# Blocks of 448 columns: sorting where PSUM is read instead of where operands are written

## The chip, the cores and the metric

The kernel runs on one core of a Trainium2 chip. The metric is the device time of one execution in microseconds (us). Three runs of the kernel before gave a median of 1079.95 us (1079.29 to 1080.52).

## The reference

```python
def _attn_ref(x, filt_r, filt_i):             # x: (2, 3008, 256)
    X = np.fft.rfft(x, axis=1)
    Y = X * (filt_r + 1j * filt_i)[None, :, :]
    return np.fft.irfft(Y, n=x.shape[1], axis=1).astype(np.float32)

def _moe_ref(x, w_in, w_out):                 # x: (6016, 256), w_in: (256, 2048), w_out: (2048, 256)
    h = x @ w_in
    g = np.where(h > 0.0, h, np.exp(np.minimum(h, 0.0)) - 1.0)
    return g @ w_out

def _moe2_ref(x, w_in, w_out):
    h = x @ w_in
    g = h * np.clip(h + 3.0, 0.0, 6.0) / 6.0
    return g @ w_out

# reference: x -> _attn_ref -> rows (6016, 256) -> _moe_ref -> _moe2_ref
```

A circular convolution over each of two sequences of 3008 rows, and then two two-layer networks, with an ELU and with a hard swish between their layers. The weights come as float64 and everything is float32.

## The kernel before

**Transforms.** The transform of 3008 = 47 x 64 points is done as matmuls: a step of 47 points (s1), one of 64 (s2), the product with the filter (`mult`, L203 to L211), and the two steps back (i2, i1). The first sequence is transformed in the prologue with float32 matmuls. The second sequence's transform runs beside the first network: there s1, s2 and i2 split each operand into a high and a low part (`split_in`, L957) and do three matmuls (`mm3`, L83 to L86: high x high, low x high, high x low). These read their moving operand contiguously: 16 x 3 matmuls in s1, 12 x 3 in s2 and 12 x 3 in i2. Their banks are read by `s1_evac` (L185), `mult` (L208, L209) and `i2_evac` (L222).

**Blocks.** The 6016 tokens stand as columns: twelve blocks, per sequence five of 512 and one of 448 (blocks 5 and 11). The 2048 hidden units are 16 chunks of 128. In the first network blocks 0 to 2 run side by side, then blocks 3, 4, 5, 6 and 11 one after the other (`SINGLES`), then the pairs (7, 8) and (9, 10). The second network runs six pairs; the last is (5, 11), the only one that is 448 wide. A single block's chunk is one unit: two halves of the first layer (`g1`), the ELU on its bank (L499 to L503), the split of its result (`g_split`, L506), and two output halves (`g2`), 12 matmuls in all. `g2` of a unit comes three units behind its `g1`. A pair's step takes two chunks for two blocks with seven products in place of eight (`prod`), evacuates them (`copy`, L631; `add`, L637), applies the function (`relu`, L648; `gate`, L658), splits (`high`, L668; `low`, L673) and multiplies with the second layer's weights (`second`). Each round of 16 chunks is eight such groups.

**Splits.** Every moving operand is split: ScalarE copies it into a rounded high part, VectorE subtracts that to get the low part. The lines are L101 and L102 for single blocks and block inputs, L105 (in `moved`) with L567 and L673 for pairs, L80 and L81 for transforms.

**Reading in pairs.** The network's matmuls read their moving operand with `shuffled`: element 0, element n/2, element 1, element n/2 + 1 and so on. In a 512 block the result is left in that order: it passes through four layers, and the output pass (L609 to L619) undoes it by reading a bank in steps of 16. In a 448 block order is kept at every layer: the split writes its halves in steps of n/2 (`paired`, `placed`), so that reading in pairs gives the original order, and banks are read contiguously.

**What sets the order.** Each engine takes its instructions in the order in which the program lists them. The list is written by hand: a prologue string, then a loop over units with lists of jobs before and after each (`pre`, `post`). The conversion of the weights from float64 (`w_words`, `w_parts`, `w_sums`) is a chain of small steps spread over the units by a budget (`pace`); it fills VectorE.

Of the kernel before, what the change touches and what calls it, by code (L numbers as in the profile page):

```python
# [23 lines left out]
P = 128  # L24
# [3 lines left out]
KP = 96  # L28
# [19 lines left out]
def fft_conv_moe_moe2(ctx, tc, xp, fq, sg, cs1, cs1t, cs2, ci2, ci1, ident, w1i, w1o, w2i, w2o, out):  # L48
# [42 lines left out]
    def shuffled(t, n=2):  # L91
        return t.rearrange("p (a b) -> p b a", a=n)
# [11 lines left out]
    def moved(t, src, **kw):  # L104
        nc.scalar.activation(placed(t), paired(src), AF.Copy, **kw)  # L105
# [70 lines left out]
    def s1_mm(b, h, jq, parts):  # L176
        accs[h, jq] = bank()
        mm3(accs[h, jq][:KP], *(m[:KP] for m in mats["s1r"]), *parts, True, True)
# [17 lines left out]
    def s2_mm(b, h, g, parts=None):  # L196
# [3 lines left out]
        else:  # L200
            mm3(accs[h, g], *mats["s2r"], *parts, True, True)

    def mult(b, h, g):  # L203
        acc, f = accs.pop((h, g)), filt.pop((b, h, g))
        u, v = t2([P, 512]), t2([P, 512])
        for c in range(2):
            a, o = slice(64 * c, 64 * c + 64), slice(64 - 64 * c, 128 - 64 * c)
            nc.vector.tensor_tensor(out=v[o], in0=acc[a], in1=flat(f[a, 1]), op=ALU.mult)  # L208
        nc.vector.tensor_tensor(out=u, in0=acc, in1=flat(f[:, 0]), op=ALU.mult)  # L209
# [3 lines left out]
    def i2_mm(b, h, g, parts=None):  # L213
# [3 lines left out]
        else:  # L217
            mm3(accs[h, g], *mats["i2r"], *parts, True, True)

    def i2_evac(b, h, g):  # L220
        o = t2([P, 4, P])
        nc.scalar.activation(flat(o), accs.pop((h, g)), AF.Copy)  # L222
# [246 lines left out]
    def x_split(layer, blk, h):  # L469
# [5 lines left out]
        split_to(hi[:, h, :n], lo[:, h, :n], src[:, h, :n])  # L475
# [3 lines left out]
    def g1_half(u, c):  # L479
# [4 lines left out]
        if c == 0:  # L484
# [3 lines left out]
            shuffled(hi[:, c, :n]), shuffled(lo[:, c, :n]), c == 0, c == 1,  # L488
        )

    def g1(u):
        l, blk, f = u
        n = BLOCKS[blk % 6]
        if u not in begun:
            g1_half(u, 0)
        g1_half(u, 1)
        acc = begun.pop(u)
        r = t2([P, 512])
        nc.scalar.activation(r[:, :n], acc[:, :n], AF.Relu, scale=-1.0)  # L499
        nc.scalar.activation(r[:, :n], r[:, :n], AF.Exp, scale=-1.0)  # L500
        nc.vector.scalar_tensor_tensor(  # L501
            out=r[:, :n], in0=r[:, :n], scalar=-1.0, in1=acc[:, :n], op0=ALU.add, op1=ALU.max
        )  # L503
        gs[u] = r

    def g_split(u):  # L506
        n = BLOCKS[u[1] % 6]
        gh, gl = t2([P, 512], F32R), t2([P, 512], F32R)
        split_to(gh[:, :n], gl[:, :n], gs[u][:, :n])
        gs[u] = gh, gl  # L510

    def g2(u):
# [7 lines left out]
        for c in range(2):  # L520
            s = slice(256 + c * P, 256 + (c + 1) * P)
            mm3(o[c][:, :n], w[:, 0, s], w[:, 1, s], shuffled(gh[:, :n]), shuffled(gl[:, :n]), f == 0, f == NF - 1)
# [3 lines left out]
        nc.scalar.activation(t[:, 0, :n], o[0][:, :n], AF.Copy)  # L526
        nc.vector.tensor_copy(t[:, 1, :n], o[1][:, :n])
# [47 lines left out]
    def prod(l, p, q, m, acc, start):  # L575
# [8 lines left out]
        mm3(acc[:, :n], w[:, 0], w[:, 1], shuffled(x[:, 0, :n]), shuffled(x[:, 1, :n]), start, True, True)  # L584

    def second(l, p, q, i, k, d, g):
        n = WIDTHS[l, p]
        if (l, p, k, d) not in outs:
# [4 lines left out]
            outs[l, p, k, d][:, :n], w[:, 0, s], w[:, 1, s], shuffled(g[0][:, :n]), shuffled(g[1][:, :n]),  # L593
# [612 lines left out]
```

## Time and profile before

| | |
|---|---|
| median of three runs | 1079.95 us |
| the profiled execution | 1081.07 us |
| its span | 1079.3 us |
| TensorE (PE) busy | 98% |
| VectorE (DVE) busy | 89% |
| ScalarE (ACT) busy | 78% |
| GpSimd (POOL) busy | 11% |
| granted TensorE clock | 0.998 |

The span goes from the first to the last instruction of one execution that the hardware profiler took; the execution's own time has a little around it. PE is TensorE's matmuls, DVE is VectorE, ACT is ScalarE, POOL is GpSimd; L102 is line 102 of the kernel. Matmuls overlap each other and their ends are modelled, so PE's busy share says little of how near it is to its peak: the distance from one start to the next does. A group's mean can hide several shapes, so the rows below keep shapes apart.

### The profile page before, as it was taken

To read this page: it belongs to the slowest core of one execution; us is meant where nothing else is said; L and a number is where in the kernel's file an instruction comes from. 1 tells how busy PE (TensorE), PEld (TensorE's weight loads), DVE (VectorE), ACT (ScalarE), POOL (GpSimd) and SP (SyncE) were. 2 spreads that over 40 slices of the span, in tenths; PEclk is the share of its full clock that TensorE was granted. 3 is DMA by queue.
4 is the path that set the end of the run, shared out by engine and by line. 5 is a ranking of instruction groups with operands and counts; after the bars stand their busy time and mean duration, and the time that the engine had idled before them with its cause. 6 is when DMAs were issued, how large, how long until landed. Compare 5 with 4: busy or idle time off the path is not lost.

```text
span 1079.3 us, 14368 instructions
## 1 busy us (share of the span) xinstructions
PE 1054.7 (98%) x5022; PEld 908.5 (84%) x5022; DVE 955.6 (89%) x1530; ACT 840.9 (78%) x1453; POOL 116.9 (11%) x115
## 2 busy tenths in 40 slices
PE   9999999999999999999989999999999999999998
PEld 6688888888799888888878788888888888888996
DVE  4899999999999999999989998888888888888876
ACT  3588887987688889888878866877777777777886
POOL 4600000036530000000111000010010010000000
PEclk9999999999999999999999999999999999999999
DMA  9992000465536323511466441200100100100100
GB/s 299 299 306 79 16 15 1 155 201 176 171 123 224 115 98 117 173 49 50 155 218 192 158 156 40 79 1 24 56 20 20 39 18 18 39 1 1 40 1 35
DMA packets 57944, 107.31 MB, mean 99 GB/s; under 512 B 5008, under 2 KB 33680, under 8 KB 57872
## 3 DMA queue, kind: packets, MB, share of 16 engines
q1 hardware_dynamic: 52144, 88.21, 24.8%
q0 software_dynamic: 4896, 17.83, 5.3%
q8 instruction: 39, 0.64, 0.3%
q10 hardware_dynamic: 832, 0.36, 0.1%
q14 instruction: 33, 0.27, 0.1%
HBM read 69.42 MB, written 36.96 MB: 99 GB/s over the span
## 4 chain that ended last, share of the span: by engine, by line
PE 36%; DVE 18%; ACT 9%; issue 3%; DMA 2%; SPq 0%; POOL 0%; DVEq 0%; POOLq 0%; ACTq 0%
PE ps L86 12%; PE ps L84 12%; PE ps L85 12%; DVE t L673 5%; DVE t L637 4%; ACT t L105 2%; DVE t L660 2%; DVE t L102 2%; ACT t L650 2%; ACT t L651 1%; DVE t L658 1%; ACT t L648 1%; DVE t L501 1%; DMA t<-scrx 1%; DVE t L567 1%
## 5 line engine op out<-in xcount | busy, mean ns | idle before, releaser
L86 PE MATMUL ps<-t,w 128*128 128x512 f32 (+1 forms) x1216 | 458.9, 377 | 6.4 <-DVE t L102 5.4
L84 PE MATMUL ps<-t,w 128*128 128x512 f32 (+1 forms) x1216 | 457.6, 376 | 1.5 <-DVE t L501 1.0
L85 PE MATMUL ps<-t,w 128*128 128x512 f32 (+1 forms) x1216 | 456.0, 375 | 0.2 <-DVE w L316 0.2
L86 PEld LDWEIGHTS ps<-t,w 128*128 128x128 f32 x1216 | 230.0, 189 | 44.2 <-DVE t L102 12.7
L84 PEld LDWEIGHTS ps<-t,w 128*128 128x128 f32 x1216 | 230.1, 189 | 30.4 <-DVE t L501 2.1
L85 PEld LDWEIGHTS ps<-t,w 128*128 128x128 f32 x1216 | 230.1, 189 | 28.7 <-DVE w L316 1.6
L105 ACT ACTIVATE t<-t 128x512 fp32r<-128x512 f32 (+1 forms) x312 | 201.7, 672 | 14.0 <-DVE t L658 10.3
L673 DVE TENSOR_TENSOR t<-t,t 128x512 fp32r<-128x512 f32 (+1 forms) x256 | 186.9, 746 | 23.2 <-ACT t L105 21.3
L648 ACT ACTIVATE t<-t,three 128x512 f32<-128x512 f32 (+1 forms) x144 | 97.3, 708 | 57.4 <-DVE t L637 56.9
L631 ACT ACTIVATE t<-ps 128x512 f32<-128x512 f32 (+1 forms) x192 | 112.6, 587 | 36.9 <-PE ps L86 36.2
L637 DVE TENSOR_TENSOR t<-ps,t 128x512 f32<-128x512 f32 (+1 forms) x192 | 128.0, 677 | 4.7 <-ACT t L631 3.6
L658 DVE SCALAR_TENSOR_TENSOR t<-t,t 128x512 f32<-128x512 f32 (+1 forms) x144 | 97.5, 703 | 33.3 <-ACT t L648 33.0
L102 DVE TENSOR_TENSOR t<-t,t 128x512 fp32r<-128x512 f32 (+1 forms) x144 | 121.3, 845 | 1.4 <-ACT t L101 1.4
L101 ACT ACTIVATE t<-t 128x512 fp32r<-128x512 f32 (+1 forms) x144 | 102.2, 716 | 10.3 <-DVE t L501 7.7
L499 ACT ACTIVATE t<-ps 128x512 f32<-128x512 f32 (+1 forms) x128 | 74.1, 579 | 22.1 <-PE ps L86 21.4
L501 DVE SCALAR_TENSOR_TENSOR t<-t,ps 128x512 f32<-128x512 f32 (+1 forms) x128 | 84.9, 664 | 6.2 <-ACT t L500 5.3
L500 ACT ACTIVATE t<-t 128x512 f32<-128x512 f32 (+1 forms) x128 | 79.3, 619 | 4.0
L84 PE MATMUL ps<-t,t 128*128 128x512 f32 (+1 forms) x160 | 61.7, 386 | 5.1 <-ACT t L631 4.1
L85 PE MATMUL ps<-t,t 128*128 128x512 f32 (+1 forms) x160 | 60.4, 377 | 0.0
L86 PE MATMUL ps<-t,t 128*128 128x512 f32 (+1 forms) x160 | 60.4, 377 | 0.0
L144 POOL TENSOR_TENSOR t<-t,sg 128x512 f32<-128x512 f32 x24 | 29.7, 1241 | 177.8 <-DMA t<-in_fq 177.8
L658 DVE SCALAR_TENSOR_TENSOR t<-t,ps 128x512 f32<-128x512 f32 (+1 forms) x48 | 32.4, 675 | 12.9 <-ACT t L648 12.8
(103 smaller groups left out, 1194.1 us busy)
## 6 DMA issues: line engine op xcount, KB each, us to landing
t<-in_fq SPq DMA_DIRECT2D x24, 512.0 KB, 6.3
scrw<-t SPq DMA_DIRECT2D x16, 512.0 KB, 3.0
w<-scrw POOLq DMA_DIRECT2D x16, 512.0 KB, 4.4
t<-in_xp SPq DMA_DIRECT2D x16, 384.0 KB, 5.8
scr<-t SPq DMA_DIRECT2D x24, 256.0 KB, 3.2
t<-scr SPq DMA_DIRECT2D x16, 384.0 KB, 5.5
scrx<-t SPq DMA_DIRECT2D x10, 512.0 KB, 3.0
t<-scr POOLq DMA_DIRECT2D x10, 512.0 KB, 5.2
```

Source lines behind the costliest of these rows:

```text
L84: nc.tensor.matmul(acc, wh, xh, start=start, stop=False, skip_group_check=more)
L85: nc.tensor.matmul(acc, wl, xh, start=False, stop=False, skip_group_check=more)
L86: nc.tensor.matmul(acc, wh, xl, start=False, stop=stop, skip_group_check=more)
L101: nc.scalar.activation(placed(hi), paired(src), AF.Copy)
L102: nc.vector.tensor_tensor(out=placed(lo), in0=paired(src), in1=_f32(placed(hi)), op=ALU.subtract)
L105: nc.scalar.activation(placed(t), paired(src), AF.Copy, **kw)
L501: nc.vector.scalar_tensor_tensor(out=r[:, :n], in0=r[:, :n], scalar=-1.0, in1=acc[:, :n], op0=ALU.add, op1=ALU.max)
L631: nc.scalar.activation(t[:, : self.n], bank_[:, : self.n], AF.Copy)
L637: nc.vector.tensor_tensor(out=self.h[key][:, :n], in0=bank_[:, :n], in1=u[:, :n], op=ALU.add)
L648: nc.scalar.activation(r[:, :n], h, AF.Relu, bias=three)
L658: stt(out=r, in0=r, scalar=6.0, in1=h, op0=ALU.min, op1=ALU.mult)
L673: nc.vector.tensor_tensor(out=placed(gl[:, :n]), in0=paired(g[:, :n]), in1=_f32(placed(gh[:, :n])), op=ALU.subtract)
```

## The change

Splits of 448 blocks no longer place anything: they read and write contiguously, as those of 512 do. The matmuls read in pairs as before, so a 448 bank now holds its columns in paired order. Whoever reads such a bank sorts it: it reads the bank in steps of two (`got`, through `sorted_`) and writes two contiguous halves (`like`, through `halves_of`). In the output pass a 448 bank is read in steps of two in place of one.

In the second sequence's transform s1, s2 and i2 read their operands in pairs as well (`map(pairs, parts)`), and `s1_evac`, `mult` and `i2_evac` sort where they read. The first sequence's transform stays as it was. Each engine's list of instructions is the same before and after, in kind, number and order, as are all DMAs; only access patterns differ.

```diff
-    def paired(t, n=2):
-        return t if t.shape[-1] == 512 else t.rearrange("p (b a) -> p b a", a=n)
-    def placed(t):
-        return t if t.shape[-1] == 512 else shuffled(t)
-    def split_to(hi, lo, src):
-        nc.scalar.activation(placed(hi), paired(src), AF.Copy)
-        nc.vector.tensor_tensor(out=placed(lo), in0=paired(src), in1=_f32(placed(hi)), op=ALU.subtract)
+    def pairs(t):
+        return t.rearrange("p (a b) -> p b a", a=2)
+    def sorted_(t, k=2):
+        return t.rearrange("p (b a) -> p a b", a=k)
+    def halves_of(t, k=2):
+        return t.rearrange("p (a b) -> p a b", a=k)
+    def got(acc, n):
+        return acc[:, :n] if n == 512 else sorted_(acc[:, :n])
+    def like(t, n):
+        return t[:, :n] if n == 512 else halves_of(t[:, :n])
...
-            mm3(accs[h, g], *mats["s2r"], *parts, True, True)
+            mm3(accs[h, g], *mats["s2r"], *map(pairs, parts), True, True)
     def mult(b, h, g):
...
+        if b:
+            acc, parted = sorted_(acc), halves_of
...
-        nc.vector.tensor_tensor(out=u, in0=acc, in1=flat(f[:, 0]), op=ALU.mult)
+        nc.vector.tensor_tensor(out=parted(u), in0=acc, in1=parted(flat(f[:, 0])), op=ALU.mult)
...
     def g1(u):
...
-        acc = begun.pop(u)
-        r = t2([P, 512])
-        nc.scalar.activation(r[:, :n], acc[:, :n], AF.Relu, scale=-1.0)
-        nc.scalar.activation(r[:, :n], r[:, :n], AF.Exp, scale=-1.0)
+        acc = got(begun.pop(u), n)
+        t = t2([P, 512])
+        r = like(t, n)
+        nc.scalar.activation(r, acc, AF.Relu, scale=-1.0)
+        nc.scalar.activation(t[:, :n], t[:, :n], AF.Exp, scale=-1.0)
...
     def g_split(u):
-        split_to(gh[:, :n], gl[:, :n], gs[u][:, :n])
+        split(gh[:, :n], gl[:, :n], gs[u][:, :n])
...
         def copy(self, bank_):
-            nc.scalar.activation(t[:, : self.n], bank_[:, : self.n], AF.Copy)
+            nc.scalar.activation(like(t, self.n), got(bank_, self.n), AF.Copy)
...
         def high(self, key):
-            moved(gh[:, : self.n], g[:, : self.n])
+            nc.scalar.activation(gh[:, : self.n], g[:, : self.n], AF.Copy)
         def low(self, key):
-            nc.vector.tensor_tensor(
-                out=placed(gl[:, :n]), in0=paired(g[:, :n]), in1=_f32(placed(gh[:, :n])), op=ALU.subtract
-            )
+            nc.vector.tensor_tensor(out=gl[:, :n], in0=g[:, :n], in1=_f32(gh[:, :n]), op=ALU.subtract)
```

## Rows read from the trace of the kernel before

**Rows 1.** The page's first part: busy us, share of the span, instructions.
```profile
PE 1054.7 (98%) x5022; PEld 908.5 (84%) x5022; DVE 955.6 (89%) x1530; ACT 840.9 (78%) x1453; POOL 116.9 (11%) x115
```

**Rows 2.** Stretches (start:end, length, then each engine's busy us and instructions).
```profile
core 0: us, PE busy (x) PEld busy (x) DVE busy (x) ACT busy (x) POOL busy (x), PEclk, DMA share, GB/s
60.00:285.00 225.00, 223.78 (x1054) 192.01 (x1053) 214.29 (x350) 186.21 (x330) 34.27 (x25) 1.00 0.37 119
285.00:297.40 12.40, 10.64 (x46) 7.99 (x45) 12.18 (x14) 7.21 (x14) 6.73 (x5) 1.00 0.66 202
297.40:362.20 64.80, 62.82 (x372) 59.71 (x371) 62.57 (x103) 55.91 (x108) 8.11 (x6) 1.00 0.49 158
362.20:396.20 34.00, 34.00 (x158) 29.40 (x157) 33.69 (x62) 29.63 (x50) 0.00 (x0) 1.00 0.42 144
396.20:445.10 48.90, 46.30 (x227) 41.38 (x226) 47.94 (x82) 43.22 (x72) 1.78 (x3) 1.00 0.37 129
700.00:900.00 200.00, 200.00 (x928) 175.14 (x927) 165.10 (x250) 146.45 (x249) 15.07 (x11) 1.00 0.07 24
```

**Rows 3.** PE's timeline in the last pair: start, us, instruction.
```profile
1008.48 0.35 PE L84 MATMUL ps<-t,w 128*128 128x448 f32 x1
...
1017.94 0.35 PE L86 MATMUL ps<-t,w 128*128 128x448 f32 x1
...
1027.08 0.35 PE L86 MATMUL ps<-t,w 128*128 128x448 f32 x1
```

**Rows 4.** Waits of PE from 297 to 363, and its timeline about the longest.
```profile
PE ps L86 <- DVE t L102: 2.0, 3, 0.8
...
330.56 0.35 PE L85 MATMUL ps<-t,w 128*128 128x448 f32 x1
...
331.96 0.35 PE L84 MATMUL ps<-t,w 128*128 128x448 f32 x1
```

**Rows 5.** Groups by form (xcount, busy us, mean ns, idle before): the splits of 448.
```profile
L105 ACT ACTIVATE t<-t 128x448 fp32r<-128x448 f32 x39 | 37.9, 1019 | 3.8 <-DVE t L658 3.8
...
L102 DVE TENSOR_TENSOR t<-t,t 128x448 fp32r<-128x448 f32 x36 | 38.5, 1069 | 0.3 <-ACT t L101 0.3
...
L673 DVE TENSOR_TENSOR t<-t,t 128x448 fp32r<-128x448 f32 x32 | 30.5, 994 | 8.7 <-ACT t L105 8.7
```

**Rows 6.** Groups by form: contiguous passes of 448.
```profile
L500 ACT ACTIVATE t<-t 128x448 f32<-128x448 f32 x32 | 18.5, 577 | 1.0
...
L658 DVE SCALAR_TENSOR_TENSOR t<-t,t 128x448 f32<-128x448 f32 x24 | 14.2, 614 | 5.2 <-ACT t L648 5.2
```

**Rows 7.** Groups by form: reads of PSUM, plain and in steps, and L300's of SBUF.
```profile
L617 DVE TENSOR_SCALAR t<-ps 128x512 f32<-128x512 f32 x10 | 6.9, 686 | 0.1
...
L637 DVE TENSOR_TENSOR t<-ps,t 128x512 f32<-128x512 f32 x168 | 113.9, 686 | 4.7 <-ACT t L631 3.6
...
L619 ACT ACTIVATE t<-ps 128x512 f32<-128x512 f32 x10 | 5.9, 592 | 0.3
...
L631 ACT ACTIVATE t<-ps 128x512 f32<-128x512 f32 x168 | 99.2, 590 | 35.6 <-PE ps L86 35.0
...
L300 DVE SCALAR_TENSOR_TENSOR t<-raw,t 128x512 f32<-128x512 uint32 x32 | 25.4, 794 | 0.7
```

**Rows 8.** PE's timeline at a transform product of the second sequence.
```profile
284.18 0.39 PE L84 MATMUL ps<-t,s_h 128*128 128x512 f32 x1
...
284.88 0.38 PE L84 MATMUL ps<-t,w 128*128 128x512 f32 x1
```

**Rows 9.** Timeline of ACT and DVE at the end: the last group's splits.
```profile
1069.15 1.81 ACT L105 ACTIVATE t<-t 128x448 fp32r<-128x448 f32 x2 [0.17 <-DVE t L658]
...
1070.18 1.81 DVE L673 TENSOR_TENSOR t<-t,t 128x448 fp32r<-128x448 f32 x2
...
1073.51 0.97 DVE L673 TENSOR_TENSOR t<-t,t 128x448 fp32r<-128x448 f32 x1 [1.06 <-ACT t L105]
```

More of the change, by code (lines that the diff above doesn't have):

```diff
@@ L177, in s1_mm @@
         accs[h, jq] = bank()
-        mm3(accs[h, jq][:KP], *(m[:KP] for m in mats["s1r"]), *parts, True, True)
+        mm3(accs[h, jq][:KP], *(m[:KP] for m in mats["s1r"]), *map(pairs, parts), True, True)
     s1o = {}
@@ L217, in i2_mm @@
         else:
-            mm3(accs[h, g], *mats["i2r"], *parts, True, True)
+            mm3(accs[h, g], *mats["i2r"], *map(pairs, parts), True, True)
     def i2_evac(b, h, g):
         o = t2([P, 4, P])
-        nc.scalar.activation(flat(o), accs.pop((h, g)), AF.Copy)
+        acc = accs.pop((h, g))
+        if b:
+            nc.scalar.activation(halves_of(flat(o)), sorted_(acc), AF.Copy)
+        else:
+            nc.scalar.activation(flat(o), acc, AF.Copy)
         nc.sync.dma_start(by_a(scr2[b][h], g), o)
@@ L474, in x_split @@
         hi, lo = xs[layer, blk]
-        split_to(hi[:, h, :n], lo[:, h, :n], src[:, h, :n])
+        split(hi[:, h, :n], lo[:, h, :n], src[:, h, :n])
     begun = {}
@@ L487, in g1_half @@
             begun[u][:, :n], w[:, 0, c * P : (c + 1) * P], w[:, 1, c * P : (c + 1) * P],
-            shuffled(hi[:, c, :n]), shuffled(lo[:, c, :n]), c == 0, c == 1,
+            pairs(hi[:, c, :n]), pairs(lo[:, c, :n]), c == 0, c == 1,
         )
@@ L496, in g1 @@
         g1_half(u, 1)
[L497 to L504 removed]
+        acc = got(begun.pop(u), n)
[3 more added lines that the diff above has]
+        nc.scalar.activation(t[:, :n], t[:, :n], AF.Exp, scale=-1.0)
+        nc.vector.scalar_tensor_tensor(out=r, in0=r, scalar=-1.0, in1=acc, op0=ALU.add, op1=ALU.max)
+        gs[u] = t
     def g_split(u):
@@ L521, in g2 @@
             s = slice(256 + c * P, 256 + (c + 1) * P)
-            mm3(o[c][:, :n], w[:, 0, s], w[:, 1, s], shuffled(gh[:, :n]), shuffled(gl[:, :n]), f == 0, f == NF - 1)
+            mm3(o[c][:, :n], w[:, 0, s], w[:, 1, s], pairs(gh[:, :n]), pairs(gl[:, :n]), f == 0, f == NF - 1)
         if f < NF - 1:
@@ L566, in x_low @@
         hi, lo = (ops[l, p, m][:, i, :n] for i in range(2))
-        nc.vector.tensor_tensor(
-            out=placed(lo), in0=paired(x_source(l, p, m)), in1=_f32(placed(hi)), op=ALU.subtract
-        )
+        nc.vector.tensor_tensor(out=lo, in0=x_source(l, p, m), in1=_f32(hi), op=ALU.subtract)
     def x_part(l, p, m):
@@ L583, in prod @@
         x = ops[l, p, m]
-        mm3(acc[:, :n], w[:, 0], w[:, 1], shuffled(x[:, 0, :n]), shuffled(x[:, 1, :n]), start, True, True)
+        mm3(acc[:, :n], w[:, 0], w[:, 1], pairs(x[:, 0, :n]), pairs(x[:, 1, :n]), start, True, True)
     def second(l, p, q, i, k, d, g):
@@ L592, in second @@
         mm3(
-            outs[l, p, k, d][:, :n], w[:, 0, s], w[:, 1, s], shuffled(g[0][:, :n]), shuffled(g[1][:, :n]),
+            outs[l, p, k, d][:, :n], w[:, 0, s], w[:, 1, s], pairs(g[0][:, :n]), pairs(g[1][:, :n]),
             q == 0 and i == k, q == NF // 2 - 1 and i != k,
@@ L636, in add @@
             self.h[key] = t2([P, 512])
-            nc.vector.tensor_tensor(out=self.h[key][:, :n], in0=bank_[:, :n], in1=u[:, :n], op=ALU.add)
+            nc.vector.tensor_tensor(out=like(self.h[key], n), in0=got(bank_, n), in1=like(u, n), op=ALU.add)
             if not self.l and key == (0, 1):
@@ L647, in relu @@
             if self.l:
-                nc.scalar.activation(r[:, :n], h, AF.Relu, bias=three)
+                nc.scalar.activation(like(r, n), h, AF.Relu, bias=three)
             elif key != (0, 1):
-                nc.scalar.activation(r[:, :n], h, AF.Relu, scale=-1.0)
+                nc.scalar.activation(like(r, n), h, AF.Relu, scale=-1.0)
                 nc.scalar.activation(r[:, :n], r[:, :n], AF.Exp, scale=-1.0)
```

38 lines of the change are left out of this document (18 added, 20 removed).

## The prediction

> **What bounds the kernel now.** I read the page's first part, then the table of stretches, then PE's own timeline. TensorE is busy 98% of the span [rows 1], but a busy PE is not yet a PE at its peak: matmuls overlap, so their spacing has to be read. Paired 512-column matmuls start every 200.00/928 = 0.2155 us in the stretch 700 to 900 [rows 2]; 448-column ones every (1017.94 - 1008.48)/50 = 0.189 us where nothing waits [rows 3]. Held against that spacing, most of the kernel has nothing to win. The reader is to see two exceptions in [rows 2]. From 297 to 362 and from 396 to 445, where the single blocks of 448 run, VectorE (DVE) is busy 62.57 of 64.80 and 47.94 of 48.90 us: DVE sets the pace and TensorE waits for it. From 996 on (the last pair, both of 448) no engine is full, and the loss there is a chain between engines.
>
> How much is lost in the second of those stretches: 227 matmuls, of which 16 chunks x 12 = 192 are 448 wide and 35 are 512 wide, would take 192 x 0.189 + 35 x 0.2155 = 43.8 us and took 48.9, so 5.1 us. In the first the profile names three waits of TensorE for L102, 2.0 us of idle time [rows 4]. Such a wait costs more than its idle time, because idle time is counted from the modelled end of a matmul that lasts longer than its spacing: two matmuls from 330.56 to 331.96 took 1.40 us in place of 0.38, so 1.02 lost for the longest wait, which the row calls 0.8. With 0.27 us more for each, 2.0 + 3 x 0.27 = 2.8 us. In the last pair a group of four steps has (7 products + 8 second-layer products) x 3 = 45 matmuls, 8.51 us, and takes 1027.08 - 1017.94 = 9.14 [rows 3]: 0.63 lost in each of 6 groups, 3.8 us.
>
> **What the change does, and its price.** Each engine's sequence of instructions stays as it was: nothing moves and no wait is added. Only access patterns change, in three ways.
>
> *The splits.* Splits of 448 wrote their halves 224 elements apart. That makes ScalarE's (ACT) copy 1019 ns (L105) and DVE's subtraction 1069 (L102) and 994 (L673) [rows 5]. Contiguous passes of the same size are 577 ns on ACT (L500) and 614 on DVE (L658) [rows 6]. So each split sheds about 0.44 us on ACT and 0.38 on DVE; I take DVE's from L673, the lower of the two means. There are 36 splits at L101/L102 and some 39 at L105 with L567 and L673. A split beside a GpSimd operation may shed less; those are few (GpSimd is busy 8.11 and 1.78 us in the two stretches) [rows 2].
>
> *The evacuations.* Every read of a 448 bank now takes every second float of PSUM, and so do the second sequence's three kinds of transform bank. No row shows a step of two in PSUM. The nearest are the output passes, which already read a 512 bank in steps of 16 floats: 686 ns on DVE against 686 for plain reads (L617, L637), 592 on ACT against 590 (L619, L631) [rows 7]. That is nothing. The other end is the price of the strided write itself, +0.38 on DVE and +0.44 on ACT. Between them lies a step of two in SBUF: L300 takes 794 ns where 512 contiguous take 686, so +0.11 [rows 7]. A price below nothing is excluded, the plain reads being as fast as the contiguous form gets. I take zero, because L617 and L619 are the same memory, the same engines and a wider step.
>
> [...]
>
> *The transforms.* 120 matmuls of the second sequence (48 of the first step, 36 and 36 of the two others) read contiguously, and start (284.88 - 284.18)/3 = 0.233 us apart [rows 8]; in pairs they should take 0.2155. That is 0.018 x 120 = 2.1 us if TensorE sets the pace. It does until about 285; 25 of the 120 lie after it, where DVE does, and 12 in the prologue. The other 83 give 1.5 us.
>
> [...]
>
> **What of it reaches the end.**
> - Before 297: from 285 to 297.4 DVE is full (12.18 of 12.40) [rows 2]. Two of block 5's input splits fall there and shed 0.4 us each: 0.7 us.
> - Block 5: DVE sheds 16 x 0.38 = 6 us where 2.8 us are lost. All 2.8.
> - Block 11: DVE sheds 18 x 0.38 = 6.8 us with the two input splits, and falls to 41.1 us of some 44. Is that enough? From 362 to 396 DVE is busy 33.69 of 34.00 and TensorE 34.00 of 34.00: at 99% DVE still keeps up when the work is even. So most of the 5.1; I leave 0.3 for uneven bunches: 4.8 us.
> - The last pair: the chain that holds TensorE up runs through one L105 and one L673 per place and gets 0.8 us shorter; the loss per group is 0.63 in all. TensorE takes over: 3.8 us.
> - The tail: three splits behind each other. Before: L105 ends its pair at 1070.96, L673's pair ends at 1071.99, the last L673 at 1074.48 [rows 9]. Stepping the shorter durations through the same order, the first L673 ends at 1070.8, the second at 1071.4, the last gate at 1071.95, its copy at 1072.5 and the last L673 at 1073.15. That is 1.3 earlier, of which TensorE's own work leaves 1.2.
>
> Sum: 1.5 + 0.7 + 2.8 + 4.8 + 3.8 + 1.2 = 14.8 us. The profiled execution took 1081.07 us with a span of 1079.3; it goes to 1066.3. It stands 1.1 us above the median of the runs, 1079.95, so the median goes to 1065.1, and I say 1065. What is late next is TensorE's own spacing, and from 445 on the waits of the 512 pairs, on which the change has no hold. Once TensorE is the bound the rest of what ACT and DVE shed is worth nothing: some 30 us go from each and only half of that reaches the end.
>
> **Rivals.**
> 1. *Reading PSUM in steps of two costs as in SBUF.* +0.11 on DVE (a little more on ACT) takes the split's gain from 0.38 to 0.27, and the 36 multiply passes of the second sequence (L208, L209) add 4 us to a DVE that has 225.00 - 214.29 = 10.7 us free over 60 to 285 [rows 2]. Bunched, about 1.5 of them show. Blocks 5 and 11 would give 5.5 instead of 7.6, the last pair and the tail 4, the rest 0.5, and the transforms 1.5 - 1.5: 10 us, so 1070. [...] Against it: L617.
> 2. *The slow side: a step of two in PSUM costs as much as the strided write did*, +0.38 on DVE. In the 448 blocks there is about one such read for each split, on either engine, so these stages gain nothing. In the second sequence's transforms 36 x 0.38 = 14 us come on top of DVE, in the last 80 us or so before 300; with 5% of them free (10.7 of 225), 4 us, some 10 us would show, less the 1.5 of the matmuls: 1088. It decides from a price of about 0.25 us per read, where the two sides cancel. For it: no row has this step. Against it: the wider step is free on both engines. [...]
> 3. *The wait only changes its name.* In blocks 5 and 11 weight conversion is placed between the splits, and TensorE may wait for its bunches in place of L102, the more so as those wait for DMA. If half of the two blocks' 7.6 us, all before 297, and the tail stay, 14.8 - 3.8 - 0.7 - 1.2 leaves 9.1: 1071. For it: DVE stays above 90% busy. Against it: 362 to 396.
> 4. *Nothing to measure*: the paths cancel or a transfer late in the kernel moves against it: within 1079.95 +/- 2.2.
>
> **How the numbers follow.** The forecast 0.74, with its own range 1061 to 1068 (from all of the 5.1, of the 2.1 and more of what is lost before 297, down to two thirds of the blocks' terms). Rival 1: 0.07, rival 3: 0.10, rival 4: 0.03, rival 2: 0.06. The range 1060 to 1072 takes in the forecast, with a us below it for waits after 445 that shorter lags may shrink, and rivals 1 and 3 as far as they reach. No change is within 0.2%, about what a measurement of this kernel can tell: 0.03. Faster: 0.74 + 0.07 + 0.10 = 0.91. Slower: 0.06.
>
> **What would show it.** In the profile after: splits of 448 at about 0.57 (ACT) and 0.61 (DVE); evacuations of 448 and multiply passes as long as before; second-sequence matmuls spaced as all others; groups of the last pair 8.5 us long; DVE below 95% in block 11 and no wait for the splits. I am wrong if a stepped PSUM read is longer than a plain one, or if DVE's shed time shows up as idle time while TensorE waits as long as before.

## The result and the profile after

The changed kernel takes 1065.82 us (median of 4 runs, 1063.73 to 1066.44) where the kernel before, run beside it, takes 1079.74 (4 runs). The ratio is 0.9867, with a 95% interval of 0.985 to 0.9884. The forecast was 1065.0 with a range of 1060 to 1072, so time and range held. The sum behind it holds in three of its six terms, fails in the two before 297 us and is too small in the tail; beside these stands a gain in the trace that I had not foreseen.

The profiled execution of the kernel after took 1063.73 us with a span of 1062.0. The first row below is the page's first part and answers to [rows 1]: TensorE is as busy as it was, and ACT sheds 27 us, near the 30 that the prediction gave, DVE only 20. DVE's rows for the splits ([rows 5], L567's, and those below) shed 27 us too, but neighbouring passes on DVE overlap (two L673 in a row take 1.81 us in [rows 9], a single one 0.97; two L680 in a row 1.15, a single one 0.62), so its busy time falls by less.

```profile
PE 1045.5 (98%) x5022; PEld 909.1 (86%) x5022; DVE 936.0 (88%) x1530; ACT 813.8 (77%) x1453; POOL 116.9 (11%) x115
```

The stretches answer to [rows 2]. Each stage is cut, to within 0.2 us, at the same matmul as before (the first of 448 columns of a block, the first of 512 behind its last ones), so the lengths can be compared.

```profile
core 0: us, PE busy (x) PEld busy (x) DVE busy (x) ACT busy (x) POOL busy (x), PEclk, DMA share, GB/s
285.00:296.90 11.90, 10.25 (x43) 7.52 (x42) 11.68 (x13) 7.20 (x14) 6.68 (x5) 1.00 0.64 195
296.90:358.70 61.80, 61.80 (x371) 59.88 (x370) 58.95 (x104) 50.16 (x108) 8.12 (x6) 1.00 0.53 168
358.70:392.60 33.90, 33.90 (x159) 29.71 (x159) 33.59 (x62) 29.66 (x52) 0.00 (x0) 1.00 0.40 140
392.60:436.80 44.20, 44.03 (x225) 41.90 (x224) 43.03 (x81) 37.29 (x71) 1.79 (x3) 1.00 0.41 142
```

In block 5 TensorE is now busy 61.80 of 61.80 us and in block 11 44.03 of 44.20; the waits of [rows 4] have no row left in the view of waits. DVE stays at 97% in block 11, where I had looked for less than 95. The prediction took 18 splits off its 47.94 us and came to 41.1; the block's two input splits start before the stage, at 390.4 and 393.2 us before and at 386.5 and 389.0 after, so 16 are left, and DVE is busy 43.03 us of a shorter stage. It holds nothing up there.

Next are the groups by form: two splits on ACT and two on DVE (they answer to [rows 5]), then the passes that read PSUM in steps of two (they answer to [rows 7]: L634 and L640 are L631 and L637 of before, for 448 columns; L506 and L508 are the first and the last pass of the ELU, L499 and L501 before).

```profile
L80 ACT ACTIVATE t<-t 128x448 fp32r<-128x448 f32 x36 | 20.4, 566 | 4.5 <-DVE t L508 4.2
L675 ACT ACTIVATE t<-t 128x448 fp32r<-128x448 f32 x32 | 17.6, 569 | 1.1 <-DVE t L665 1.1
L81 DVE TENSOR_TENSOR t<-t,t 128x448 fp32r<-128x448 f32 x36 | 25.7, 714 | 0.0
L680 DVE TENSOR_TENSOR t<-t,t 128x448 fp32r<-128x448 f32 x32 | 19.2, 620 | 3.1 <-ACT t L675 3.0
...
L508 DVE SCALAR_TENSOR_TENSOR t<-t,ps 128x448 f32<-128x448 f32 x32 | 19.7, 616 | 1.8 <-ACT t L507 1.8
L640 DVE TENSOR_TENSOR t<-ps,t 128x448 f32<-128x448 f32 x24 | 14.4, 622 | 5.1 <-ACT t L634 5.1
L506 ACT ACTIVATE t<-ps 128x448 f32<-128x448 f32 x32 | 17.2, 536 | 1.0 <-PE ps L86 1.0
L634 ACT ACTIVATE t<-ps 128x448 f32<-128x448 f32 x24 | 13.0, 543 | 11.1 <-PE ps L86 9.9 <-ACT t L675 0.6
...
L211 DVE TENSOR_TENSOR t<-ps,t 128x512 f32<-128x512 f32 x24 | 16.6, 692 | 0.5
```

The same passes of 448 columns in the trace of before, where they read PSUM plainly:

```profile
L501 DVE SCALAR_TENSOR_TENSOR t<-t,ps 128x448 f32<-128x448 f32 x32 | 19.6, 614 | 0.9 <-ACT t L500 0.9
L637 DVE TENSOR_TENSOR t<-ps,t 128x448 f32<-128x448 f32 x24 | 14.2, 614 | 0.0
L499 ACT ACTIVATE t<-ps 128x448 f32<-128x448 f32 x32 | 17.3, 542 | 0.1
L631 ACT ACTIVATE t<-ps 128x448 f32<-128x448 f32 x24 | 13.4, 560 | 1.3 <-PE ps L86 1.1
```

ACT's split goes from 1019 to 566 and 569 ns, DVE's from 994 to 620 (L680) and from 1069 to 714 (L81). The last two are means that mix: four of the 36 splits run beside GpSimd and take 1.81 to 1.85 us before, 1.46 to 1.49 after; the others take about 0.97 before and 0.62 after. The stepped reads cost nothing: the same passes took 614 and 614 ns on DVE, 542 and 560 on ACT before, and take 616, 622, 536 and 543. The multiplication of the second sequence (L211, L209 before) has a mean of 692 ns in both. That settles the choice of zero for the unknown price.

In the last pair a group of 45 matmuls takes 8.51 us where [rows 3] showed 9.14, and the view of waits has no row for TensorE in the whole pair. PE's timeline, one group apart:

```profile
1015.67 0.35 PE L86 MATMUL ps<-t,t 128*128 128x448 f32 x1
...
1024.18 0.35 PE L86 MATMUL ps<-t,t 128*128 128x448 f32 x1
```

At a transform product of the second sequence [rows 8] gave a spacing of 0.233 us; after, four matmuls in PE's timeline give (284.33 - 283.68)/3 = 0.217:

```profile
283.68 0.38 PE L84 MATMUL ps<-t,s_h 128*128 128x512 f32 x1
...
284.33 0.38 PE L84 MATMUL ps<-t,w 128*128 128x512 f32 x1
```

**Where the time went, stage by stage** (kernel time to the same matmul in the two traces; the first and last matmul of the pair are at 995.92 and 1075.21 us before, and at 984.58 and 1057.86 after; the tail is the pair's last 33 matmuls):

| stage | before | after | gain | forecast |
|---|---|---|---|---|
| start to block 5 | 297.42 | 296.92 | 0.5 | 1.5 + 0.7 |
| block 5 | 64.9 | 62.0 | 2.9 | 2.8 |
| to the end of block 11 | 82.9 | 78.1 | 4.8 | 4.8 |
| 512 pairs | 550.7 | 547.6 | 3.1 | 0 |
| last pair, up to the tail | 70.9 | 67.0 | 3.9 | 3.8 |
| tail, to the last matmul | 8.4 | 6.25 | 2.1 | 1.2 |

Of the third row, block 11 itself gives 4.5 us. The 0.5 of the first row isn't clear of what two traces differ by: the kernel with the last pair's edit alone, which is the kernel before up to there, comes to that matmul at 298.05. The two traces are 17.3 us apart; the medians differ by 13.9, because the profiled execution of before stands 1.3 us above its median and that of after 2.1 below. The row that doesn't belong to the change is the fourth, and the section on why comes back to it.

### The profile page after: what moved, and what is told of

It is laid out like the page before. It is cut to its first block, busy times and chain, and to the rows that moved or that the text cites. A ratio compares the mean times of both kernels' runs of the same rounds, so it can differ in the third digit from the quotient of the medians.

```text
span 1062.0 us, 14390 instructions
## 1 busy us (share of the span) xinstructions
PE 1045.5 (98%) x5022; PEld 909.1 (86%) x5022; DVE 936.0 (88%) x1530; ACT 813.8 (77%) x1453; POOL 116.9 (11%) x115
## 4 chain that ended last, share of the span: by engine, by line
PE 69%; DVE 16%; ACT 7%; issue 4%; DMA 2%; POOL 1%; SPq 0%; DVEq 0%; POOLq 0%; ACTq 0%
PE ps L84 21%; PE ps L86 21%; PE ps L85 21%; DVE t L680 3%; DVE t L640 2%; PE ps L241 2%; DVE t L81 2%; DVE t L508 2%; DVE t L667 2%; ACT t L656 1%; PE ps L154 1%; ACT t L657 1%; POOL t L213 1%; DMA t<-scrx 1%; PE ps L198 1%
## 5 line engine op out<-in xcount | busy, mean ns | idle before, releaser
L680 DVE TENSOR_TENSOR t<-t,t 128x512 fp32r<-128x512 f32 (+1 forms) x256 | 175.7, 700 | 18.0 <-ACT t L675 16.4
L675 ACT ACTIVATE t<-t 128x512 fp32r<-128x512 f32 (+1 forms) x256 | 154.3, 616 | 8.4 <-DVE t L665 7.2
L634 ACT ACTIVATE t<-ps 128x512 f32<-128x512 f32 (+1 forms) x192 | 112.0, 583 | 48.8 <-PE ps L86 47.2
L640 DVE TENSOR_TENSOR t<-ps,t 128x512 f32<-128x512 f32 (+1 forms) x192 | 128.6, 679 | 10.6 <-ACT t L634 9.6
L81 DVE TENSOR_TENSOR t<-t,t 128x512 fp32r<-128x512 f32 (+2 forms) x172 | 133.5, 780 | 2.4 <-ACT t L80 1.5
L80 ACT ACTIVATE t<-t 128x512 fp32r<-128x512 f32 (+2 forms) x184 | 109.8, 608 | 31.9 <-POOL t L213 23.1
L506 ACT ACTIVATE t<-ps 128x512 f32<-128x512 f32 (+1 forms) x128 | 73.9, 577 | 24.6 <-PE ps L86 24.2
L508 DVE SCALAR_TENSOR_TENSOR t<-t,ps 128x512 f32<-128x512 f32 (+1 forms) x128 | 85.0, 664 | 6.3 <-ACT t L507 6.0
```

The lines of the kernel that those rows point to most:

```text
L80: nc.scalar.activation(hi, src, AF.Copy)
L81: eng.tensor_tensor(out=lo, in0=src, in1=_f32(hi), op=ALU.subtract)
L508: nc.vector.scalar_tensor_tensor(out=r, in0=r, scalar=-1.0, in1=acc, op0=ALU.add, op1=ALU.max)
L634: nc.scalar.activation(like(t, self.n), got(bank_, self.n), AF.Copy)
L640: nc.vector.tensor_tensor(out=like(self.h[key], n), in0=got(bank_, n), in1=like(u, n), op=ALU.add)
L675: nc.scalar.activation(gh[:, : self.n], g[:, : self.n], AF.Copy)
```

## The experiments

Eleven kernels ran. In all of them "before" is the kernel before, timed on the same chip; an experiment's own file numbers its lines otherwise where a helper was added or taken out.

**The two halves of the change by themselves.** The first kernel keeps the 448 edit and reads and evacuates the second sequence's transforms as before (in the other two transform steps likewise):

```
-        mm3(accs[h, jq][:KP], *(m[:KP] for m in mats["s1r"]), *map(pairs, parts), True, True)
+        mm3(accs[h, jq][:KP], *(m[:KP] for m in mats["s1r"]), *parts, True, True)
```

> The edit to the 448 blocks alone; the second sequence's transforms read contiguously and are read plainly, as before. Theory (contiguous splits carry nearly all of the 13.9 us): 12 to 13 us below before, 1067 to 1068, last pair and block 11 without waits as in the whole change. Rival (the paired transforms carry a good share, since they shorten TensorE's stretch beside a full DVE): 1071 or more.

Measured: 1064.9 us (1064.67 to 1066.63), ratio 0.9867 (0.9854 to 0.988). That is 2 us below what I had expected: the whole gain is there without the transforms.

The second kernel is the kernel before with the transforms' edit alone:

```
-            mm3(accs[h, g], *mats["s2r"], *parts, True, True)
+            mm3(accs[h, g], *mats["s2r"], *map(pairs, parts), True, True)
```

> The edit to the transforms alone; 448 splits as before. Theory: the 120 matmuls are 0.018 us closer to each other, but where DVE is full by then the gain is waited away: 0.5 to 1.5 us below before, 1078.3 to 1079.3. Rival: 3 us or more below (1076.7), since every us counts. If a step of two in PSUM cost anything, the 36 multiply passes would be longer than 0.689 us and the time above before.

Measured: median 1079.97 us of 12 runs (1078.27 to 1088.44), ratio 1.0008 (0.9994 to 1.0023). This half is worth nothing that can be measured, though its matmuls do start closer (3.24 us from one product to the next where the kernel before has 3.29). The profiled execution took 1088.44 us: its first matmuls start 0.21 us apart in place of 0.11, so it is 8.1 us behind by the matmul that starts at 15.9 us before, ahead of the transforms, and 7.6 at the first matmul of block 5. The multiplications are no longer than before (689 and 692 ns), so the rival that taxes PSUM reads can't be the reason. My expectation of 0.5 to 1.5 us was wrong.

**Reads or writes?** The split's old form read in order and wrote its halves 224 floats apart. Two kernels change only how the loop runs. The first goes over the same pairs of addresses in the other order: it reads every second float and writes two runs of 224.

```
-        return t if t.shape[-1] == 512 else t.rearrange("p (b a) -> p b a", a=n)
+        return t if t.shape[-1] == 512 else t.rearrange("p (b a) -> p a b", a=n)
-        return t if t.shape[-1] == 512 else shuffled(t)
+        return t if t.shape[-1] == 512 else t.rearrange("p (a b) -> p a b", a=2)
```

> The kernel before with the loops of the 448 splits swapped: the same elements go to the same places, but each split reads every second float of SBUF and writes two runs of 224, where it read in order and wrote 224 apart. Theory (the write far apart is the dear part, a read in steps of two costs what L285 and L300 showed): splits 0.73 to 0.75 us on ACT and 0.70 to 0.73 on DVE in place of 1.02 and 0.97, and two thirds of the blocks' gain: 1069 to 1073. Rival (either pattern with two loops is dear): splits stay near 1.0 and the time within 1 us of before.

Measured: 1066.87 us (1065.71 to 1067.2), ratio 0.988 (0.9867 to 0.9893). Its groups by form:

```profile
L105 ACT ACTIVATE t<-t 128x448 fp32r<-128x448 f32 x39 | 24.7, 654 | 1.1 <-DVE t L658 1.1
...
L673 DVE TENSOR_TENSOR t<-t,t 128x448 fp32r<-128x448 f32 x32 | 19.2, 621 | 3.4 <-ACT t L105 3.4
...
L567 DVE TENSOR_TENSOR t<-t,t 128x448 fp32r<-128x448 f32 x7 | 5.2, 748 | 0.0
```

In L673 DVE pays nothing for reading every second float (621 against 620 contiguous; I had expected 700 to 730), ACT 0.085 us (654 against 569). In the seven splits of the pair's inputs, L567, the same pattern takes 748 ns against 620, so it isn't free everywhere; what sets the two apart wasn't looked into. The time is below the 1069 to 1073 that I had expected: 13.0 us are to be had by swapping two letters in each of two access patterns, with no PSUM read touched.

The mirror of it reads two runs and writes every second float. It leaves the columns of a 448 block in another order, so what it computes there is not the reference's:

```
-        return t if t.shape[-1] == 512 else t.rearrange("p (b a) -> p b a", a=n)
+        return t if t.shape[-1] == 512 else t.rearrange("p (a b) -> p a b", a=n)
-        return t if t.shape[-1] == 512 else shuffled(t)
+        return t if t.shape[-1] == 512 else t.rearrange("p (b a) -> p a b", a=2)
```

> The kernel before, its 448 splits reading two runs of 224 and writing every second float, so that a 448 block's columns come in another order. Theory (a write is dear only where neighbours land far apart; a step of two is like the reads in steps of two): splits at 0.65 us or less on ACT and 0.75 or less on DVE, 1066 to 1070. Rival (every write that isn't contiguous costs the same): 1.0 us on both and the time of before, 1078 to 1081.

Measured: 1066.51 us (1065.89 to 1066.53), ratio 0.9876 (0.9863 to 0.9889), and by form:

```profile
L105 ACT ACTIVATE t<-t 128x448 fp32r<-128x448 f32 x39 | 24.6, 654 | 1.0 <-DVE t L658 1.0
...
L673 DVE TENSOR_TENSOR t<-t,t 128x448 fp32r<-128x448 f32 x32 | 19.3, 624 | 3.5 <-ACT t L105 3.5
...
L567 DVE TENSOR_TENSOR t<-t,t 128x448 fp32r<-128x448 f32 x7 | 5.4, 796 | 0.0
```

Writing in steps of two floats is about as cheap as reading so (L567 pays 0.05 us more). What costs 0.37 us on DVE and 0.45 on ACT is that neighbouring elements are written 224 floats apart. The old DVE pass also read its high part 224 apart; the next kernel reads everything in order and writes far apart, and its split takes 973 ns against 994, so only some 0.02 of the 0.37 lies with that read. Far reads by themselves were not run.

**Which engine's half binds where.** Two kernels put the far writes back on one engine only, on all 448 splits, in the kernel after. For DVE:

```
-        nc.vector.tensor_tensor(out=lo, in0=x_source(l, p, m), in1=_f32(hi), op=ALU.subtract)
+        nc.vector.tensor_tensor(out=placed(lo), in0=paired(x_source(l, p, m)), in1=paired(_f32(hi)), op=ALU.subtract)
```

> The changed kernel, but the subtractions of the 448 splits (VectorE's half) write 224 apart again, while ScalarE's copies stay contiguous; the low parts of 448 blocks stand at other places, so the 448 blocks' values are not the reference's. Theory (in blocks 5 and 11 VectorE sets the pace; in the last pair both halves lie on the chain): most of the blocks' gain is lost and some of the pair's, 7 to 10 us above the changed kernel, 1073 to 1076. Rival (ScalarE's copy was what held TensorE up): 3 us or less above, 1069 or below.

Measured: 1073.74 us (1072.08 to 1074.48), ratio 0.9945 (0.9932 to 0.9957), 7.9 above the kernel after. Its L690 and L114 are the splits of [rows 5], and the window is block 11 to within a us:

```profile
L690 DVE TENSOR_TENSOR t<-t,t 128x448 fp32r<-128x448 f32 x32 | 29.8, 973 | 1.6 <-ACT t L685 0.6
...
L114 DVE TENSOR_TENSOR t<-t,t 128x448 fp32r<-128x448 f32 x36 | 38.3, 1065 | 0.0
...
396.40:444.90 48.50, 46.04 (x225) 41.24 (x224) 47.69 (x81) 38.11 (x72) 1.78 (x3) 1.00 0.38 131
```

DVE is at 47.69 of 48.50 us as in [rows 2], with ACT 5 us freer, and TensorE is at 46.04 again. Between the same matmuls block 5 takes 64.3 us and block 11 48.7: of their gains of 2.9 and 4.5 us 2.3 and 4.3 are undone. The last pair takes 74.2 us, only 0.9 longer than after, all of it in the tail.

The copies of ACT in the same way:

```
-            nc.scalar.activation(ops[l, p, m][:, 0, :n], x_source(l, p, m), AF.Copy)
+            nc.scalar.activation(placed(ops[l, p, m][:, 0, :n]), paired(x_source(l, p, m)), AF.Copy)
```

> The other half: ScalarE's copies of the 448 splits write 224 apart again, VectorE's subtractions stay contiguous; the high parts of 448 blocks stand at other places, so the 448 blocks' values are not the reference's. Theory: blocks 5 and 11 keep nearly all of their gain, the pair's groups lose 0 to 0.2 us each and the tail about 1: 1 to 3 us above the changed kernel, 1067 to 1069. Rival (ScalarE's copy holds TensorE up): 7 us or more above, 1073 or more.

Measured: 1068.03 us (1066.98 to 1070.67), ratio 0.9898 (0.9885 to 0.9912), 2.2 above after. L685 is ACT's split of the last pair:

```profile
L685 ACT ACTIVATE t<-t 128x448 fp32r<-128x448 f32 x32 | 30.9, 1020 | 0.9 <-DVE t L675 0.8
...
396.40:444.90 48.50, 47.60 (x238) 44.05 (x236) 46.10 (x86) 45.79 (x78) 1.79 (x3) 1.00 0.39 137
```

A split as dear as before on ACT costs block 11 one us (45.5 us in all) and the last pair 0.6 (73.9, all of it in the tail). Against my expectation it also costs block 5 2.4 us in this trace (64.4): TensorE waits 1.1 us for a DVE split there, in a stretch where ACT is full (2.97 of 3.00 us from 352.6 to 355.6). The profiled execution took 1070.67 us, 2.6 above the median of four, so how much of this the other executions have stays open. So DVE's half binds in block 11; in block 5 either half's far writes brought most of the wait back. In the last pair either engine alone gives more than 5 of the 6 us: up to the tail both kernels take 67.0 us as after, so some 0.4 us off the chain is enough there, and the change takes off 0.8.

**The last pair by itself.** Here only the pair's two blocks have the new order; the single blocks and the transforms are as before. Beside the old helper, this takes the four edits of the evacuations of a single block back, as in

```
-        acc = got(begun.pop(u), n)
+        acc = begun.pop(u)[:, :n]
```

> The edit to the last pair of 448 alone (second network); single blocks 5 and 11 and the transforms as before. Theory: the pair's groups fall from 9.14 to 8.51 us and the tail gets shorter, 5 to 6 us below before, 1074 to 1075. Rival (TensorE's waits in the pair move to another place): 2 us or less, 1077.7 or more.

Measured: 1073.66 us (1072.99 to 1074.32), ratio 0.9944 (0.9933 to 0.9956): 6.2 us less than before, where the trace's balance has 6.0 for the pair with its tail and the forecast 5.0. The stage's worth is its own: it isn't lent from the blocks ahead.

**Why the transforms gave nothing.** From about 278 to 297 us TensorE waits for DVE. Two explanations were open: DVE's subtractions stand while GpSimd works (L81 is 1.70 us beside it and 0.68 alone), or DVE simply has too much of its own to do. One kernel moves the 12 subtractions of one transform input from GpSimd to DVE, which adds work to DVE and takes the neighbour away:

```
-        pre[t - 1].insert(0, lambda: split_in(("z", h, g), flat(zs[1, h, g]), nc.gpsimd))
+        pre[t - 1].insert(0, lambda: split_in(("z", h, g), flat(zs[1, h, g]), nc.vector))
```

> The changed kernel with the twelve subtractions of the z split moved from GpSimd to VectorE. Before 297 two units take 8.32 us whatever the splits cost; VectorE's L81 takes 1.70 us beside GpSimd's and 0.68 alone. Theory (VectorE stands still while GpSimd reads): 0.68 more work for 1.0 less standing, two units take about 8.0, 1 to 2 us below the changed kernel, 1064 to 1065. Rival (it is VectorE's own work that fills the 8.32): two units take about 9.0, 1 to 3 us above, 1067 to 1069.

Measured: 1069.25 us (1068.36 to 1070.01), ratio 0.9906 (0.9892 to 0.9919), 3.4 above after. DVE is busy 96.36 of the 100 us from 200 to 300, as after (96.51), while GpSimd falls from 42.49 to 26.78: DVE does 6 instructions more in the same busy time, so its work grew by about as much as its standing fell. The stretch on which the two explanations part comes out as the first has it: two products take 7.97 us (GpSimd's sum starts at 280.27, 288.24 and 296.21) where they took 8.32. But from about 253 on, where TensorE had set the pace, a product takes 3.4 and 4.0 us in turn in place of 3.24, so the time went the second one's way, a little past its 1 to 3 us.

The other takes GpSimd's sign products away, and gives them to ACT in four pieces of 128 columns:

```
+        if b:
+            for k in range(4):
+                nc.scalar.activation(fi[:, k, :], fi[:, k, :], AF.Copy, scale=mats["sg"][:, 4 * g + k : 4 * g + k + 1])
+            return
         nc.gpsimd.tensor_tensor(out=fi, in0=fi, in1=s, op=ALU.mult)
```

> The changed kernel with the second sequence's sign products (GpSimd L143, 1.49 us each beside VectorE) done on ScalarE as four products of 128 columns each. Theory (VectorE stands still while GpSimd reads): L81 loses about 1 us once in two units, which then take about 7.4 us in place of 8.32, and TensorE's 3.9 us of loss from 278 to 297 shrink to 1 to 2: 2 to 3 us below the changed kernel, 1063 to 1064. Rival (the loop through TensorE, VectorE, GpSimd and ScalarE is what takes 8.32, or ScalarE's four products come in the way): within 0.5 us of it or above.

Measured: 1075.42 us (1074.89 to 1078.84), ratio 0.9962 (0.9948 to 0.9975), 9.6 above after. The window from 200 to 300 us, first of after and then of this kernel:

```profile
200.00:300.00 100.00, 97.91 (x448) 82.75 (x447) 96.51 (x133) 78.23 (x144) 42.49 (x31) 1.00 0.57 179
```

```profile
200.00:300.00 100.00, 94.58 (x419) 76.52 (x418) 81.75 (x125) 84.56 (x176) 23.33 (x18) 1.00 0.55 173
```

DVE's busy time falls by 15 us, and 8 fewer instructions at some 0.7 us are under 6 of them: the standing beside GpSimd is real. Yet TensorE does 29 matmuls fewer. What took DVE's place is ACT's list. ACT's timeline, with one row of DVE's:

```profile
271.25 0.63 ACT L80 ACTIVATE t<-t 128x512 fp32r<-128x512 f32 x1 [1.73 <-POOL t L217]
271.79 1.26 ACT L145 ACTIVATE t<-t,sg 128x128 f32<-128x128 f32 x4
272.95 0.57 ACT L510 ACTIVATE t<-ps 128x512 f32<-128x512 f32 x1
...
274.22 0.69 DVE L512 SCALAR_TENSOR_TENSOR t<-t,ps 128x512 f32<-128x512 f32 x1 [1.62 <-ACT t L511]
```

ACT waits 1.73 us for GpSimd's sum, then does the sign pieces ahead of the copy that the next layer's DVE pass needs, and DVE stands 1.62 us. Two products now take 7.86 us (ACT's L80 starts at 263.39, 271.25 and 279.11) where the end of the stretch took 8.3, but they take that from 238 on, where GpSimd's sums came 6.75 us apart. So the theory's premise holds, its price doesn't: the time came out on the rival's side, with ACT's products in the way. Neither kernel made the way to block 5 shorter; that DVE's standing beside GpSimd is what keeps the transforms' gain from it is argued and not shown.

**The load that lay in the way in the trace of before.** One kernel starts the loads of the second network's inputs one step earlier in the list of later work:

```
-        (2, 2, x2_load, 0), (2, 2, x2_load, 1), (3, 2, x_sums, 0), (4, 0, x_high, 1),
+        (1, 2, x2_load, 0), (1, 2, x2_load, 1), (3, 2, x_sums, 0), (4, 0, x_high, 1),
```

> The changed kernel with the two loads of a round's inputs (x2_load of the rounds after the first) placed four units earlier. In the trace of before TensorE stood 2.92 us at 561.7 for a load from scrx that took 11.4 us, and its clock then fell for 3.4 us; the changed kernel's trace has no such wait, though its other runs took 2 us longer than the profiled one. Theory (that wait comes in most runs and not in that one): 1 to 2.5 us below the changed kernel's median, 1063.3 to 1064.8, and no wait for scrx. Rival (the profiled run is the usual one, or the earlier tiles make other transfers wait): within 0.7 us of it or above.

Measured: 1063.67 us (1063.12 to 1072.46, 6 runs), ratio 0.9864 (0.9841 to 0.9888), 2.1 below after by the medians, with intervals that overlap. In the trace of after DVE's first pass on the input of the second network's first pair still waits (the row is from 530 to 600 us); in this kernel's it doesn't:

```profile
L556 DVE TENSOR_TENSOR t<-t,t 128x512 f32<-128x512 f32 x3 | 2.1, 689 | 1.2 <-DMA t<-scrx 1.2
```

The last kernel has the same earlier loads in the first experiment's, that is, without the transforms' edit.

> The edit to the 448 blocks alone, with the loads of a round's inputs four units earlier as in the run beside it. Theory: the paired transforms are worth nothing here, so it takes the same as that run within 1 us, 1063 to 1065, the best version so far or equal to it. Rival (the paired transforms are worth 1.5 us): 1 us or more above that run.

Measured: 1063.68 us (1063.37 to 1064.28), ratio 0.9852 (0.9838 to 0.9866). The simpler kernel is as fast as the one with the transforms' edit, and both have the lowest medians of all that ran.

## Why the prediction held, and where it failed

**The price of the stepped PSUM read** was the choice on which the forecast's side hung: zero, from the output passes' steps of sixteen. It is zero (616 and 622 ns for 614 and 614, 536 and 543 for 542 and 560). With it the first two rivals fall: no stepped pass is longer, and DVE has nothing new to do. The step of two in SBUF, from which the first rival took its 0.11, turned out to cost DVE nothing in L673 (621) and 0.13 in L567 (748), and ACT 0.085.

**The splits' price** was 0.38 and 0.44 us. In the last pair it is 994 - 620 = 374 ns on DVE and 450 on ACT; on L81 it is 355. The four splits beside GpSimd, which the prediction thought might shed less, shed as much (1.83 us to 1.46).

**Blocks 5 and 11** were worked out from the spacing of matmuls and not from busy shares: 2.8 and 4.8 us forecast, 2.9 measured and 4.5 in block 11, or 4.8 with the stretch between the blocks. The third rival, that the wait would only change its name, is excluded by the view of waits, which has none left there. The experiments with far writes on one engine show DVE's half to bind in block 11 (4.3 us of 4.5 undone, against 1.0 by ACT's); in block 5 they don't tell the two apart (2.3 and 2.4 of 2.9).

**The last pair.** Up to the tail the pair gave 3.9 us for 3.8. The tail gave 2.1 for 1.2, and that term was mis-sized. I had stepped through the last three splits alone and stopped the sum at TensorE's own work. Before, TensorE needed from 1066.83 to 1075.21 us for the pair's last 33 matmuls; after, from 1051.61 to 1057.86, 6.25 us, where 32 spacings of 0.189 are 6.05: it is hardly held up to the end. Counted from the first of these 33, the first ACT copy of [rows 9] already starts 0.96 us earlier (1069.15 - 1066.83 = 2.32 before, 1052.97 - 1051.61 = 1.36 after), because the splits ahead of it got shorter too; that is what the sum left out. From there to the end of the last DVE split it is 1.17 us less, near the 1.3 of the stepping. ACT and DVE in the tail of the kernel after answer to [rows 9]:

```profile
1052.97 0.57 ACT L675 ACTIVATE t<-t 128x448 fp32r<-128x448 f32 x1
...
1055.90 0.58 ACT L675 ACTIVATE t<-t 128x448 fp32r<-128x448 f32 x1 [0.87 <-DVE t L665]
...
1054.18 1.15 DVE L680 TENSOR_TENSOR t<-t,t 128x448 fp32r<-128x448 f32 x2
...
1056.51 0.62 DVE L680 TENSOR_TENSOR t<-t,t 128x448 fp32r<-128x448 f32 x1 [0.64 <-ACT t L675]
```

Two DVE splits that lay behind each other at 1.81 us take 1.15, and the last one ends 4.8 us ahead of the span's end in both traces, so what lies behind it didn't move.

**The step that failed** is "The other 83 give 1.5 us", and with it the 0.7 us before 297. I had TensorE set the pace until about 285. The trace lets its lead be followed. At the same product it is 0.05 us at 192, grows by 0.05 with each of the products, and is 277.35 - 276.10 = 1.25 us by 277. Seven us later it is 284.18 [rows 8] - 283.68 = 0.50, and it is 0.50 at the first matmul of block 5. In PE's timeline of before and then of after:

```profile
277.35 0.40 PE L84 MATMUL ps<-t,s_h 128*128 128x512 f32 x1
```

```profile
276.10 0.38 PE L84 MATMUL ps<-t,s_h 128*128 128x512 f32 x1
...
288.81 0.48 PE L86 MATMUL ps<-t,i_h 128*128 128x512 f32 x1 [0.42 <-DVE t L81]
```

So the matmuls did gain about what I gave them, and most of it was waited away at one point. The last row shows the form of it: TensorE at a product, waiting for DVE's L81. From there on a loop through DVE and GpSimd sets the time, and the change has no hold on it. The loop ran at its own pace long before: GpSimd's sums of the multiplications start 0.45 us earlier than before at 235 us (235.48 against 235.93) and still 0.46 at 277 (276.62 against 277.08), while TensorE's lead grew to 1.25. So TensorE only ran ahead of the loop. Its pace at the end can be read from the same sums, before and then after (DVE's subtraction is the last row):

```profile
285.43 1.28 POOL L211 TENSOR_TENSOR t<-t,t 128x512 f32<-128x512 f32 x1 [2.84 <-DVE t L209]
...
293.76 1.28 POOL L211 TENSOR_TENSOR t<-t,t 128x512 f32<-128x512 f32 x1 [2.84 <-DVE t L209]
```

```profile
284.95 1.27 POOL L213 TENSOR_TENSOR t<-t,t 128x512 f32<-128x512 f32 x1 [2.83 <-DVE t L211]
...
289.15 1.28 POOL L81 TENSOR_TENSOR t<-t,t 128x512 fp32r<-128x512 f32 x1 [1.48 <-ACT t L80]
...
293.27 1.27 POOL L213 TENSOR_TENSOR t<-t,t 128x512 f32<-128x512 f32 x1 [2.84 <-DVE t L211]
...
289.28 1.70 DVE L81 TENSOR_TENSOR t<-t,t 128x512 fp32r<-128x512 f32 x1
```

8.33 us for two products before, 8.32 after. I had read DVE's 12.18 of 12.40 us as work, of which two cheaper splits would be a part. Only one of block 5's two input splits starts in that stretch (287.2 us; the other at 278.8), and it did get 0.37 us shorter, from 1.83 to 1.46. The last two rows show that part of this busy time is standing: DVE's L81 starts at 289.28 beside GpSimd's, which ends at 290.43, and ends 0.55 us behind that; alone it takes 0.68. That was open to me in the trace of before, where an L102 of 512 columns takes 1.44 us beside GpSimd's L81 (at 281.70) and 0.67 with GpSimd idle (at 364.70), and would have made me doubt the 0.7.

That the transforms are worth nothing is shown by the kernel with their edit alone (1.0008, 0.9994 to 1.0023). The forecast of the time survives because the error is 1.7 us and the tail's 0.9 us gives half of it back. That the median came out within a us of the forecast is in part luck.

**What I had not foreseen** are the 3.1 us between 445 and 996 in the trace of before. TensorE stands there, in its timeline, 2.92 us from one start to the next (DVE's row and a stretch behind it follow):

```profile
561.66 0.38 PE L86 MATMUL ps<-t,w 128*128 128x512 f32 x1
564.58 0.48 PE L84 MATMUL ps<-t,t 128*128 128x512 f32 x1 [2.54 <-ACT t L631]
...
562.08 0.69 DVE L551 TENSOR_TENSOR t<-t,t 128x512 f32<-128x512 f32 x1 [3.41 <-DMA t<-scrx]
...
565.10:568.50 3.40, 3.40 (x10) 2.74 (x9) 3.17 (x7) 3.37 (x7) 2.09 (x4) 0.56 0.68 197
```

DVE waits 3.41 us for a load of the input of the second network's first pair, ACT waits behind DVE and TensorE behind ACT. In the stretch behind it the granted clock is 0.56, and eight matmuls start 0.43 us apart in place of 0.2155, some 1.7 us in all. In the trace of after the DVE pass waits 1.2 us for the same load, TensorE takes 0.67 us from one start to the next at the same matmul, 2.25 less, and the clock stays at 1.00. Of these 3.9 us 0.8 are lost again elsewhere in the stage. The load takes up to 11.4 us from issue to landing before and 8.8 after (median 3.5 and 3.6), and nothing that the change does touches it.

The other traces tell how common the wait is. DVE waits for this load in all eleven kernels that issue it at the old place: 1.2 and 1.3 us in the traces of after and of the z split on DVE, 1.9 to 3.8 in the other nine, among them the blocks' edit alone with 2.3. It is gone in the two that issue it earlier. The clock doesn't fall behind every long wait: over the whole profiled execution it is 0.998 in before and in ACT's far writes, where DVE waits 3.4 and 3.8 us for the load, and 1.0 in the transforms' edit alone, where it waits 3.7. So the trace of after is a lucky one; its other three executions took 1.8 to 2.7 us longer, which more of this wait would fit. Without the 3.1 us the two traces would be 14.2 us apart, and the medians are 13.9; how much of the medians' difference the wait is stays open. The kernel that issues the load earlier is 2.1 us below after by the median, with intervals that overlap.

## What to carry to other kernels

Read where an engine's pass puts neighbouring elements before its count of elements: swap the two loops of an access pattern so that writes are close together and the reads pay for the order (here nothing to 0.13 us a pass in place of 0.37), and try that before anything that touches a second place. Work out a gain on TensorE from the spacing of its matmuls, stage by stage, and follow the lead at the same matmul through both traces: a lead that grows and then vanishes at one point (here 1.25 us, and 0.50 seven us later) shows that another loop sets the time there. Take a full engine's busy time for work only after holding the same instruction's duration beside a busy and beside an idle neighbour (here 1.70 us against 0.68).

## What the runs showed of the hardware

- A write whose neighbours lie 224 floats apart in SBUF makes a 448-column split 0.97 to 0.99 us on DVE and 1.02 on ACT; with contiguous writes it is 0.62 and 0.57. Steps of two floats, on the read or on the write side, cost DVE nothing in one place (621 and 624 ns) and 0.13 and 0.18 us in another (748 and 796), and ACT 0.085 (654).
- PSUM read in steps of two floats costs nothing on either engine (448 columns: 616 and 622 ns for 614 on DVE, 536 and 543 for 542 and 560 on ACT).
- fp32r matmuls of 512 columns whose moving operand is read alternately from two halves start 0.2155 us apart (0.217 in the second sequence's transform), contiguous ones 0.233.
- A DVE subtraction of 512 columns beside a GpSimd operation took 1.70 us, and 0.68 alone; one of 448 columns 1.46 and 0.62.
- The same load took 7.3 to 11.4 us from issue to landing at its longest in three traces, at a median of 3.5 to 3.6; behind the longest TensorE took 2.92 us from one start to the next, and the granted clock was 0.56 for the next 3.4 us.
